# Three rotating 8 MiB buffers, K loaded one pair ahead of V, and the work on head pairs in loops with running address registers

## The chip, the core and the metric

One core of one Trainium2 chip runs the kernel. The metric is the device time of one execution in microseconds. The kernel before takes 654.78 us, the median of six runs (654.01 to 656.37).

## What is computed

A gated mix of two branches for one token x of 512 values: attention over a cache of 32 heads with 16384 keys and values of 128 bf16 numbers each, and a small gated MLP.

```python
g = sigmoid((x * gate_w).sum(-1, keepdims=True))
q = (x @ wq).reshape(B, Sq, H, Dh).transpose(0, 2, 1, 3)      # H = 32, Dh = 128
scores = einsum('bhqd,bhkd->bhqk', q, k_cache) * Dh ** -0.5    # 16384 keys
p = softmax(scores, axis=-1)
o = einsum('bhqk,bhkd->bhqd', p, v_cache)
a = o.transpose(0, 2, 1, 3).reshape(B, Sq, H * Dh) @ wo
z = gelu(x @ w_in); z1 = z[..., :Fh]; z2 = layernorm(z[..., Fh:])
b = (z1 * (w_sp * z2 + b_sp)) @ w_out                          # one token
return g * a + (1 - g) * b
```

The two caches are 128 MiB each, so almost everything that the kernel moves is K and V, and each of their values is used once.

## The kernel before

Heads are taken in 16 pairs. A pair's K fills one buffer of 128 partitions by 64 KiB (8 MiB): head one on partitions 0 to 63, head two on 64 to 127, with 256 keys to a partition. V has the same layout. There are two K buffers (`k_buf`) and one V buffer (`v_buf`); the set-up weights wq and w_in lie in `v_buf`, w_out and a scratch area in `k_buf[1]`, and wo goes into `k_buf[0]` at the end.

For a pair i:

- VectorE multiplies K in place by the query in four chunks of 64 keys (`mult`, L362), each after the load's semaphore (first chunk) and each announced by `mul_s`.
- TensorE sums a chunk's 128 products down to 8 partial sums per key with 16 matmuls against the identity (`scores`, L322 and L74), in one of two PSUM banks. VectorE reduces the 8 to one score (`reduce`, L366).
- ScalarE takes the exponentials of both heads and their sums (`exps`, L378).
- TensorE multiplies the weights into V with 64 matmuls of 8 columns, spread over four column groups of the array (`attend`, L333). ScalarE drains the result to SBUF (L414), and four fp32 matmuls pick the two heads' columns (L339), which ScalarE saves (L416). VectorE inverts the sums (L372).

SyncE's queue issues all large loads in the order K_0, V_0, K_1, V_1, and so on. K_i waits until the scores of pair i-2 are summed (L388), V_i until the V matmuls of pair i-1 are through (L391). The last pair's loads are cut into pieces, K into two and V into three (L398, L402), and after them come five pieces of wo (L421). TensorE's program for two pairs is one loop body with all matmuls written out (L346); VectorE's and ScalarE's programs are written out for all 16 pairs. GpSimd only passes on V's semaphores.

Ahead of the pairs the queries (32 matmuls, L217), the gate, and the MLP branch (16 matmuls L251, a chain of small VectorE steps, 14 matmuls L305) are worked out while the first K loads. After them the outputs are scaled (L424 to L429), turned into columns (L433 to L439, the result is o2), and 64 matmuls of one row by 256 columns multiply by wo (L444) as its pieces land. Two copies and one store end the kernel (L450 to L454).

Of the kernel before, what the change touches and what calls it, by code (L numbers as in the profile page):

```python
# [12 lines left out]
P = 128  # L13
# [17 lines left out]
NG = KP // 4  # L31
ZB = F // 4
K_CUTS = (0, 128, 256)
V_CUTS = (0, 128, 224, 256)
WO_CUTS = (0, 16, 26, 30, 31, 32)
# [3 lines left out]
class Queue:  # L39

    def __init__(self, nc, name):
        self.sem = nc.alloc_semaphore(f"{name}_done")
        self.n = 0
        self.steps = []
# [22 lines left out]
    def issue(self, eng):  # L67
        for step in self.steps:
            step(eng)


def matmul_again(nc, eng, out, lhsT, rhs, **flags):
    with nc.discard():
        ins = eng.matmul(out, lhsT=lhsT, rhs=rhs, **flags).ins  # L74
    return eng.add_instruction(dataclasses.replace(
        ins, name=nc.get_next_instruction_name(), ldweights=False))


def advance(block, engine, n):
    todo = block.instructions  # L80
    loads = [i for i in todo if i.engine == engine and isinstance(i, mybir.InstDMACopy)][:n]
    for load in loads:
        todo.remove(load)
    at = next(j for j, i in enumerate(todo) if i.engine == engine and isinstance(i, mybir.InstDrain))
    todo[at:at] = loads


def gated_mix_kernel(nc, A_x, A_k_cache, A_v_cache, A_wq, A_wo, B_x, B_w_in, B_w_sp, B_b_sp,
# [4 lines left out]
    def ps(name):  # L93
        return nc.alloc_psum_tensor(name, [P, 512], FP32)

    k_buf = [sb(f"k_buf{b}", [P, ROW], BF16) for b in range(2)]
    v_buf = sb("v_buf", [P, ROW], BF16)
    qb = sb("qb", [P, NP * Dh], BF16)
    p_t = sb("p_t", [P, NG * 8], BF16)
    s_sb = [sb(f"s_sb{i}", [P, KP], FP32) for i in range(2)]  # L100
    d_sb = sb("d_sb", [P, 512], FP32)
    x_row = sb("x_row", [1, D], BF16)
# [3 lines left out]
    xgs = sb("xgs", [1, 1], FP32)  # L106
# [19 lines left out]
    L_sb = sb("L_sb", [P, 2], FP32)  # L126
    rl = sb("rl", [P, H], FP32)
    oa = sb("oa", [P, H], FP32)
# [4 lines left out]

    s_ps = [ps(f"s_ps{i}") for i in range(2)]
    d_ps = ps("d_ps")
    o_ps = ps("o_ps")
    l_ps = ps("l_ps")
    a_ps = ps("a_ps")
    m_ps = [ps(f"m_ps{i}") for i in range(2)]
    z_banks = [s_ps[0], s_ps[1], o_ps, l_ps]  # L140

    wq = v_buf[:, 0:DC * HDh]
    w_in = v_buf[:, DC * HDh:DC * (HDh + F)]
    w_out = k_buf[1][:, 0:FhC * D]
    zm = k_buf[1][:, FhC * D:FhC * D + 2 * F].bitcast(FP32)
    wo = k_buf[0]
# [6 lines left out]
    entry = nc.m.functions[0].blocks[0]  # L153
    fin = sem("fin")
    ld_x, ld_g, ld_q, ld_w, ld_u, ld_v, st_out = (
        sem(n) for n in ("ld_x", "ld_g", "ld_q", "ld_w", "ld_u", "ld_v", "st_out"))
    ld_k = [sem(f"ld_k{b}") for b in range(2)]
    ld_kh = [sem(f"ld_kh{b}") for b in range(len(K_CUTS) - 1)]
    ld_vp = [sem(f"ld_vp{b}") for b in range(len(V_CUTS) - 1)]
    ld_o = [sem(f"ld_o{b}") for b in range(len(WO_CUTS) - 1)]  # L160
    mul_s, red_s, sum_s, exp_s, sl_s, pv_s, drn_s, col_s = (
        sem(n) for n in ("mul_s", "red_s", "sum_s", "exp_s", "sl_s", "pv_s", "drn_s", "col_s"))

    pe, dve, act, pool, sp = (Queue(nc, n) for n in ("pe", "dve", "act", "pool", "sp"))
# [5 lines left out]
    for t in [L_sb, p_t]:  # L170
        p_zero = pool.op(lambda e, t=t: e.memset(t[:, :], 0.0), mark=True)
    ones_ok = dve.op(lambda e: e.memset(ones_row[:, :], 1.0), mark=True)
# [18 lines left out]
    for c in range(DC):  # L191
        x_ok = pe.op(lambda e, c=c: e.matmul(
            m_ps[0][:, c * P:(c + 1) * P], lhsT=x_row[0:1, c::DC], rhs=ones_row[0:1, :],
            start=True, stop=True), wait=[(ld_x, 16), ones_ok] if c == 0 else (), mark=True)
    xb_ok = dve.op(lambda e: e.tensor_copy(out=xb[:, :], in_=m_ps[0][:, :]), wait=[x_ok], mark=True)

    for i in range(4):
        dve.chain(lambda e, i=i: e.tensor_copy(
            out=sel[:, i * P:(i + 1) * P].rearrange("h (m i) -> h m i", i=4)[:, :, i],
            in_=ident[0:H, 0:H]), wait=[ident_ok])  # L200
# [6 lines left out]
    xgs_ok = dve.chain(lambda e: e.tensor_reduce(out=xgs[:, :], in_=xg_row[:, :], axis=AX.X,  # L207
                                                 op=ALU.add))

    q_banks = [*z_banks, d_ps, a_ps, m_ps[1], m_ps[0]]  # L210
    q_free = []
    for c in range(DC):
        for n in range(8):
            rhs = wq[:, c * HDh + n * 512:c * HDh + (n + 1) * 512]
            flags = dict(start=(c == 0), stop=(c == DC - 1))
            q_ok = pe.op(lambda e, n=n, c=c, rhs=rhs, flags=flags: (
                e.matmul(q_banks[n][:, :], lhsT=xb[:, c * P:(c + 1) * P], rhs=rhs, **flags)  # L217
                if n == 0 else
                matmul_again(nc, e, q_banks[n][:, :], xb[:, c * P:(c + 1) * P], rhs, **flags)),
                wait=[xb_ok, (ld_q, 16)] if c == 0 and n == 0 else (), mark=(c == DC - 1))  # L220
            if c < DC - 1:
                continue
            for s in range(2):
                rows = slice(64 * s, 64 * s + 64)
                src = q_banks[n][rows, :].rearrange("p (j two d) -> p j two d", two=2,
                                                    d=Dh)[:, :, s, :]
                dst = qb[rows, n * 256:(n + 1) * 256].rearrange("p (j d) -> p j d", d=Dh)
                if n % 2 == 0:
                    ok = dve.op(lambda e, src=src, dst=dst: e.tensor_copy(out=dst, in_=src),  # L229
                                wait=[q_ok] if s == 0 else (), mark=True)  # L230
                else:
                    ok = act.op(lambda e, src=src, dst=dst: e.copy(out=dst, in_=src),
                                wait=[q_ok] if s == 0 else (), mark=True)
            q_free.append(ok)

    pe.op(lambda e: e.matmul(m_ps[1][:, 0:1], lhsT=ones_f[0:1, :], rhs=xgs[:, :], start=True,
                             stop=True), wait=[xgs_ok, q_free[6]], mark=True)
    g_ok = pe.op(lambda e: e.matmul(m_ps[1][:, 1:3], lhsT=ones_row[0:1, :], rhs=wb_row[0:1, :],
                                    start=True, stop=True), wait=[(ld_g, 48)], mark=True)
    act.op(lambda e: e.activation(out=g_sb[:, :], in_=m_ps[1][:, 0:1], func=ACT.Sigmoid),  # L240
           wait=[g_ok], mark=True)
    gm_ok = act.op(lambda e: e.activation(out=gm_sb[:, :], in_=m_ps[1][:, 0:1], func=ACT.Sigmoid,
                                          scale=-1.0), mark=True)
    dve.op(lambda e: e.tensor_copy(out=wbf[:, :], in_=m_ps[1][:, 1:3]), wait=[gm_ok], mark=True)

    for c in range(DC):
        for n in range(4):
            rhs = w_in[:, c * F + n * ZB:c * F + (n + 1) * ZB]
            flags = dict(start=(c == 0), stop=(c == DC - 1))
            z_ok = pe.op(lambda e, n=n, c=c, rhs=rhs, flags=flags: (  # L250
                e.matmul(z_banks[n][:, 0:ZB], lhsT=xb[:, c * P:(c + 1) * P], rhs=rhs, **flags)  # L251
                if n == 0 else
                matmul_again(nc, e, z_banks[n][:, 0:ZB], xb[:, c * P:(c + 1) * P], rhs, **flags)),
                wait=[(ld_w, 16), q_free[2], q_free[3]] if c == 0 and n == 0 else (),
                mark=(c == DC - 1))
            if c == DC - 1:
                m0 = n % 2 * 64
                zb_ok = dve.op(lambda e, n=n, m0=m0: e.tensor_tensor(
                    out=zm[:, n * ZB:(n + 1) * ZB].rearrange("p (m k) -> p m k", k=FhC),
                    in0=z_banks[n][:, 0:ZB].rearrange("p (m k) -> p m k", k=FhC),  # L260
                    in1=ident[:, m0:m0 + 64].unsqueeze(2).broadcast_to([P, 64, FhC]),
                    op=ALU.mult), wait=[z_ok], mark=True)
# [17 lines left out]
    tot_ok = pe.op(lambda e: e.matmul(m_ps[1][:, 0:2], lhsT=ones_f[:, :], rhs=stats[:, :],  # L280
                                      start=True, stop=True), wait=[st_ok, gm_ok], mark=True)
    dve.op(lambda e: e.tensor_scalar(out=mv[:, :], in0=m_ps[1][:, 0:2], scalar1=1.0 / Fh,
# [7 lines left out]
                                          bias=eps_t[:, 0:1], scale=1.0), wait=[var_ok, const_ok],  # L290
                   mark=True)
# [6 lines left out]
                                        op=ALU.mult))  # L298
    u_ok = dve.chain(lambda e: e.tensor_scalar(out=u[:, :], in0=z2n[:, :], scalar1=gm_sb[:, 0:1],
                                               scalar2=0.0, op0=ALU.mult, op1=ALU.add),  # L300
                     wait=[gm_ok])
    d_zero = dve.op(lambda e: e.memset(d_ps[:, :], 0.0), wait=[q_free[4]], mark=True)
    for k in range(FhC):
        for s in range(2):
# [198 lines left out]
```

The softmax here doesn't subtract the row's maximum and nothing guards it: scores larger than these inputs give would overflow.

## Time and profile before

| | before |
|---|---|
| median of six runs | 654.78 us |
| the profiled execution | 654.27 us |
| its span, first to last instruction | 652.5 us |
| mean rate of the transfers over the span | 429 GB/s |
| VectorE multiply L362, 64 times | 282.5 us, 4416 ns each |
| TensorE score matmuls L74 and L322, 1024 times | 275.1 us |
| TensorE V matmuls L333, 1024 times | 68.6 us summed, four at a time |

Busy time is the sum of an engine's instructions. Matmuls that overlap are each counted in full, so a sum on TensorE can be more than the time they took together. The chain of waits follows the work that ended last backwards. SPq and PEq are the sequencers of SyncE and TensorE: they run waits, register operations and branches, and issue the DMAs. "Landing" is the moment at which a DMA's semaphore is complete.

### The profile page before, as it was taken

Reading aid. Unit: us, or ns where it says so; the run is one execution under the profiler, and the core shown is the slowest. Engines: PE = TensorE matmul, PEld = TensorE weight load, DVE = VectorE, ACT = ScalarE, POOL = GpSimd, SP = SyncE. Lnnn points to the kernel's source line nnn. Section 1 sums busy time; section 2 is a strip of 40 time slices with the busy share of each in tenths; the row PEclk is TensorE's granted clock in tenths of the full one; section 3 lists DMA queues with packets and bytes.
Section 4 is the critical chain, followed back from the end, with each engine's and each line's share of the span. In section 5 each row is a group of like instructions: output and inputs, shape, how many; then the busy total and the mean of one; then the engine's idle time right before and its main releaser. Section 6 shows DMA issues by size and latency. Waiting matters only on the chain. (4 is left out here: it accounts for less than half of the span.)

```text
span 652.5 us, 4336 instructions
## 1 busy us (share of the span) xinstructions
PE 374.9 (57%) x2348; PEld 64.5 (10%) x1348; DVE 338.1 (52%) x192; ACT 37.1 (6%) x112; POOL 1.2 (0%) x8
## 2 busy tenths in 40 slices
PE   2646275563837546384563747556484754638766
PEld 0000101011010200102010010101101020010103
DVE  1486290754719166380935629075471915638560
ACT  0210001000010100001010000100001010000100
POOL 0000000000000000000000000000000000000000
PEclk9859788687978959798795978869697895968897
DMA  9999999999999999999999999999999999999997
GB/s 386 478 398 450 443 438 407 442 446 442 406 442 446 430 418 442 446 418 430 442 442 410 438 446 442 410 438 442 446 402 446 442 446 402 442 446 414 426 423 292
DMA packets 6209, 279.64 MB, mean 429 GB/s; under 512 B 696, under 2 KB 956, under 8 KB 1212
## 3 DMA queue, kind: packets, MB, share of 16 engines
q1 hardware_dynamic: 6196, 279.58, 99.3%
q8 instruction: 2, 0.03, 0.0%
q14 instruction: 3, 0.02, 0.0%
q10 hardware_dynamic: 8, 0.00, 0.0%
HBM read 279.58 MB, written 0.00 MB: 429 GB/s over the span
## 5 line engine op out<-in xcount | busy, mean ns | idle before, releaser
L362 DVE TENSOR_TENSOR k_buf<-k_buf,qb 128x8192 bf16<-128x8192 bf16 x64 | 282.5, 4416 | 200.0 <-DMA k_buf<-in_A_k_cache_dram 200.0
L74 PE MATMUL s_ps<-k_buf,ident 128*128 128x512 bf16 x960 | 247.6, 416 | 0.0
L322 PE MATMUL s_ps<-k_buf,ident 128*128 128x512 bf16 x64 | 27.5, 429 | 207.0 <-PEq L315 207.0
L366 DVE TENSOR_REDUCE s_sb<-s_ps 128x64 f32<-128x512 f32 x64 | 44.1, 688 | 74.3 <-PE s_ps L74 74.3
L333 PE MATMUL d_ps<-v_buf,p_t 128*8 128x512 bf16 x1024 | 68.6, 426 | 0.7 <-PEq L330 0.7
L322 PEld LDWEIGHTS s_ps<-k_buf,ident 128*128 128x128 bf16 x64 | 6.3, 98 | 407.2 <-issue 407.2
L378 ACT ACTIVATE p_t<-s_sb 64x256 bf16<-64x256 f32 x32 | 13.3, 414 | 479.7 <-DVE s_sb L366 479.5
L333 PEld LDWEIGHTS d_ps<-v_buf,p_t 128*8 128x8 bf16 x1024 | 30.7, 94 | 30.7 <-issue 13.2
L339 PE MATMUL o_ps<-pick,d_sb 128*128 128x2 f32 x128 | 16.8, 253 | 12.5 <-PEq L337 12.5
L327 PE MATMUL l_ps<-L_sb,ones_f 128*128 128x2 f32 x32 | 5.7, 247 | 30.9 <-PEq L326 30.9
L339 PEld LDWEIGHTS o_ps<-pick,d_sb 128*128 128x128 f32 x128 | 15.9, 195 | 20.1 <-issue 20.1
L327 PEld LDWEIGHTS l_ps<-L_sb,ones_f 128*128 128x128 f32 x32 | 4.8, 188 | 87.2 <-issue 87.2
L414 ACT COPY d_sb<-d_ps 128x512 f32<-128x512 f32 x15 | 8.8, 585 | 71.9 <-PE d_ps L333 71.9
L217 PE MATMUL s_ps<-v_buf,xb 128*128 128x512 bf16 x4 | 2.0, 495 | 9.8 <-DMA v_buf<-in_A_wq_dram 9.8
L444 PE MATMUL a_ps<-k_buf,o 128*1 128x256 bf16 x64 | 5.5, 355 | 0.9 <-DMA k_buf<-in_A_wo_dram 0.9
L378 ACT ACTIVATION_READ_ACCUMULATOR p_t<-s_sb 64x1 f32 x32 | 5.9, 185 | 0.0
L229 DVE CAST qb<-s_ps 64x256 bf16<-64x256 f32 x2 | 0.8, 422 | 7.3 <-PE s_ps L217 7.2
L280 PE MATMUL m_ps<-stats,ones_f 128*128 128x2 f32 x2 | 0.6, 364 | 6.7 <-DVE stats L278 6.7
L205 DVE TENSOR_TENSOR xg_row<-x_row,gw_row 1x512 bf16<-1x512 bf16 x1 | 0.4, 413 | 7.5 <-DMA wb_row<-in_B_b_sp_dram 7.5
L74 PE MATMUL s_ps<-v_buf,xb 128*128 128x512 bf16 (+1 forms) x8 | 3.9, 487 | 0.0
L74 PE MATMUL o_ps<-v_buf,xb 128*128 128x512 bf16 (+1 forms) x8 | 3.9, 487 | 0.0
L444 PEld LDWEIGHTS a_ps<-k_buf,o 128*1 128x1 bf16 x64 | 3.5, 108 | 2.7 <-DMA k_buf<-in_A_wo_dram 1.0
(82 smaller groups left out, 51.6 us busy)
## 6 DMA issues: line engine op xcount, KB each, us to landing
k_buf<-in_A_k_cache_dram SPq DMA_DIRECT2D x2, 4096.0 KB, 39.9
v_buf<-in_A_wq_dram SPq DMA_DIRECT2D x1, 4096.0 KB, 12.2
v_buf<-in_A_v_cache_dram SPq DMA_DIRECT2D x1, 4096.0 KB, 18.5
v_buf<-in_A_v_cache_dram SPq DMA_DIRECT2D x1, 3072.0 KB, 25.4
k_buf<-in_A_wo_dram SPq DMA_DIRECT2D x1, 2048.0 KB, 31.8
v_buf<-in_B_w_in_dram SPq DMA_DIRECT2D x1, 1792.0 KB, 15.4
k_buf<-in_A_wo_dram SPq DMA_DIRECT2D x1, 1280.0 KB, 34.4
v_buf<-in_A_v_cache_dram SPq DMA_DIRECT2D x1, 1024.0 KB, 27.4
```

The lines of the kernel that those rows point to most:

```text
L74: ins = eng.matmul(out, lhsT=lhsT, rhs=rhs, **flags).ins
L217: e.matmul(q_banks[n][:, :], lhsT=xb[:, c * P:(c + 1) * P], rhs=rhs, **flags)
L229: ok = dve.op(lambda e, src=src, dst=dst: e.tensor_copy(out=dst, in_=src), wait=[q_ok] if s == 0 else (), mark=True)
L322: ins = e.matmul(args[0], lhsT=args[1], rhs=args[2], start=True, stop=False)
L327: e.matmul(l_ps[:, 0:2], lhsT=ones_f[:, :], rhs=L_sb[:, :], start=True, stop=True).then_inc(sl_s, 1)
L333: ins = e.matmul(d_ps[32 * g:32 * g + 8, :], lhsT=p_t[:, 8 * t:8 * t + 8], rhs=v_buf[:, t * 512:(t + 1) * 512], start=(t < 4), stop=(t >= ...
L339: ins = e.matmul(o_ps[:, 0:2], lhsT=d_sb[:, r * Dh:(r + 1) * Dh], rhs=pick[:, r * 2:(r + 1) * 2], start=(r == 0), stop=(r == 3))
L362: dve.op(lambda e: e.tensor_tensor(out=k3, in0=k3, in1=q3, op=ALU.mult), wait=wait, inc=(mul_s, 1))
L366: dve.op(lambda e: e.tensor_reduce(out=s_sb[i % 2][:, c * QK:(c + 1) * QK], in_=s_ps[c % 2][:, :].rearrange("p (j w) -> p j w", w=W), axis ...
L378: act.op(lambda e, s=s, rows=rows: e.activation(out=p_t[rows, :].rearrange("p (t c) -> p t c", c=8)[:, :, 4 * s:4 * s + 4], in_=s_sb[i % 2 ...
L414: act.op(lambda e: e.copy(out=d_sb[:, :], in_=d_ps[:, :]), wait=[(pv_s, i + 1), d_zero], inc=(drn_s, 1))
L444: y_ok = pe.op(lambda e, k=k, s=s: e.matmul(a_ps[32 * s:32 * s + 1, 0:256], lhsT=o2[:, k:k + 1], rhs=wo[:, k * D + s * 256:k * D + (s + 1) ...
```

## The change

K and V share three buffers in rotation. The loads run K_0, K_1, V_0, K_2, V_1, and so on to K_15, V_14, V_15, wo; load n goes into buffer n mod 3 and waits until the user of load n-3 is done. The set-up weights all lie in the third buffer. GpSimd waits for every load and hands it on through two counting semaphores, `k_s` and `v_s`.

TensorE's order becomes scores(0), scores(1), values(0), scores(2), values(1), and so on, in blocks that branch to each other. Scores run in loops of four chunks by five groups of three matmuls, values in a loop of 16 groups of four. Buffer addresses are kept in registers (`kw`, `va`, `pa`) that are advanced in the loop, with one register operation ahead of each matmul. VectorE's and ScalarE's programs for pairs are loops as well. The V matmuls now add onto a bank that is zero at the start of a pair: ScalarE drains it and then copies zeros into it (`renew`). The outputs of all pairs gather in one PSUM bank, and the softmax sums are summed over the partitions once, at the end. Before the pairs, the query and MLP matmuls are loops that add onto banks cleared by VectorE. The first 28 of wo's 32 slices are multiplied as rows of 512 columns in four column groups, then copied to SBUF and summed by two fp32 matmuls; wo comes in seven pieces.

```diff
-    k_buf = [sb(f"k_buf{b}", [P, ROW], BF16) for b in range(2)]
-    v_buf = sb("v_buf", [P, ROW], BF16)
+    bufs = sb("bufs", [P, 3 * ROW], BF16)
+    buf = [bufs[:, b * ROW:(b + 1) * ROW] for b in range(3)]
...
+    k_at = [max(2 * i - 1, 0) for i in range(NP)]
+    v_at = [min(2 * i + 2, 2 * NP - 1) for i in range(NP)]
+    setup = buf[v_at[0] % 3]
...
+    dve.op(lambda e: e.memset(ps_all[:, 0:7 * 512], 0.0), mark=True)
...
+    z_zero = dve.op(lambda e: e.memset(ps_all[:, 0:4 * 512], 0.0), wait=[q_free[3]], mark=True)
...
+    u_ok = dve.op(lambda e: e.memset(ps_all[:, 4 * 512:6 * 512], 0.0), wait=[q_free[5]], mark=True)
...
+    def scores(e, i, ka, kw):
+        take(e, exp_s)
...
+        with e.Fori(0, NQ) as c:
+            e.reg_mov(kw, ka)
+            take(e, mul_s)
...
+            with e.Fori(0, 5) as v:
+                kv = k3[:, :, bass.ds(v * (3 * W) + W, 3 * W)]
+                for w in range(3):
+                    ins = matmul_on(nc, e, lambda: matmul_again(
+                        nc, e, s3, ident[:, :], kv[:, :, w * W:(w + 1) * W], start=False, **flags),
+                        [(kw, 2 * W * (w + 1))])
+                e.reg_alu(kw, kw, 6 * W, ALU.add)
+                ins.then_inc(sum_s, 1)
...
+    def values(e, p, pa, va):
...
+        with e.Fori(0, NT) as t:
+            take(e, v_s)
+            p8 = p_t[:, bass.ds(t * (TG * 8), TG * 8)]
+            v8 = bufs[:, bass.ds(t * (TG * 512), TG * 512)]
+            for j in range(TG):
+                ins = matmul_on(nc, e, lambda: matmul_at(
+                    nc, e, d_ps, 32 * (j % 4), (8, 512), p8[:, 8 * j:8 * j + 8],
+                    v8[:, j * 512:(j + 1) * 512], (p_t[:, 0:8], bufs[:, 0:512])),
+                    [(va, 1024 * j), (pa, 16 * j)])
+            ins.then_inc(pv_s, 1)
+            e.reg_alu(va, va, 2 * TG * 512, ALU.add)
+            e.reg_alu(pa, pa, 2 * TG * 8, ALU.add)
+        take(e, drn_s)
...
+    def renew(e):
+        drain(e).then_inc(zer_s, 1)
+        take(e, zer_s)
+        e.copy(out=d_ps, in_=zero[:, :]).then_inc(drn_s, 1)
...
+    for n, kind, i in loads:
+        wait = [user[n - 3]] if n >= 3 else [w_free] if buf[n % 3] is setup else []
...
+    def hand(e, loaded, to, n):
+        take(e, loaded, 16)
+        e.nop().then_inc(to, n)
...
-WO_CUTS = (0, 16, 26, 30, 31, 32)
+WO_CUTS = (0, 8, 16, 24, 28, 30, 31, 32)
+WIDE = 28
...
+            if k < WIDE:
+                wide_ok = pe.op(lambda e, k=k: e.matmul(
+                    s_ps[0][32 * (k % 4):32 * (k % 4) + 1, :], lhsT=o2[:, k:k + 1],
+                    rhs=wo[:, k * D:(k + 1) * D], start=(k < 4), stop=(k >= WIDE - 4)), wait=wait,
+                    mark=(k == WIDE - 1))
+                continue
...
+        if b == H - 2:
+            w_ok = act.op(lambda e: e.copy(out=d_sb[:, :], in_=s_ps[0]), wait=[wide_ok], mark=True)
```

`matmul_on` emits a matmul and replaces its address arithmetic by one addition to the running register; neighbouring register operations (two additions here, one for each operand) are fused into one instruction by the compiler. `matmul_at` places a matmul on a given column group.

## The prediction

> **What bounds the kernel now.** I read the page's busy shares and queues first, then SyncE's waits, then the chain of waits, then the last 50 us in the timeline and by line.
>
> ```profile
> span 652.5 us, 4336 instructions
> PE 374.9 (57%) x2348; PEld 64.5 (10%) x1348; DVE 338.1 (52%) x192; ACT 37.1 (6%) x112; POOL 1.2 (0%) x8
> ...
> q1 hardware_dynamic: 6196, 279.58, 99.3%
> q8 instruction: 2, 0.03, 0.0%
> q14 instruction: 3, 0.02, 0.0%
> ```
>
> No engine is above 57%, while SyncE's queue keeps the 16 DMA engines at work for 99.3% of the span. The kernel is a stream of 279.58 MB. Two thin rows below it are instruction fetches, five packets in the span.
>
> ```profile
> SPq L391 <- PE d_ps L333: 522.4, 14, 40.7
> ```
>
> SyncE waits nearly always for V's buffer (the end of L333). That wait costs no transfer: the first K half of the last pair is used at 610.68 and the next V is issued at 611.63, when the second half of that K is still in flight (a K takes 47.2 us from issue to landing; pairs follow at 155.54 - 116.84 = 38.7 us in the timeline, so one K or V is 19.35). So the queue never runs dry, and a third buffer has no bubble to fill.
>
> ```profile
> 612.47 0.43 SPq L402
> 612.90 0.04 issue
> 612.95 31.82 DMA k_buf<-in_A_wo_dram
> 644.77 0.04 issue
> 644.81 5.55 PE a_ps L444 x64
> 650.36 0.02 issue
> 650.39 0.41 DVE res L450
> ```
>
> The end: wo's first piece lands at 644.77, the 64 matmuls of L444 run up to 650.36. By L421's landing times (35 us after issues up to 614.85) the last piece lands at about 649.8, so TensorE ends only 0.6 us after the stream.[...]
>
> ```profile
> 639.98 0.14 PEld L333 LDWEIGHTS d_ps<-v_buf,p_t 128*8 128x8 bf16 x8 [1.13 <-issue]
> 640.01 0.61 PE L333 MATMUL d_ps<-v_buf,p_t 128*8 128x512 bf16 x8 [0.66 <-PEq L330]
> 640.66 0.58 ACT L428 COPY d_sb<-d_ps 128x512 f32<-128x512 f32 x1 [4.93 <-PE d_ps L333]
> ...
> 644.00 0.19 DVE L439 CAST o<-m_ps 128x32 bf16<-128x32 f32 x1 [0.40 <-PE m_ps L436]
> ```
>
> V's last piece lands at 639.9 and is used within 0.7 us. From the drain to o2 is 644.2 - 640.65 = 3.6 us. One pair's 64 V matmuls take 3.63 us in the timeline (the row at 607.96): 57 ns each, since four share the array.
>
> ```profile
> L346 PEldq ALU_OP  x8: 36/36/39, 108.0 to 641.4; - x8
> L346 PEldq COMPARE_BRANCH  x8: 76/208/214, 108.1 to 641.5; - x8
> ```
>
> These rows (the line of the old loop) hold the prices of the new loops: a register operation runs 36 ns, a taken branch 208 ns. In the trace the branch starts 97 ns after the register operation before it started, so one register operation occupies the sequencer for 97 ns. A semaphore wait there (L315, L326) runs 51 ns and the next instruction starts 75 ns after it.
>
> [...]
>
> **The change, part by part.**
>
> 1. Load order and buffers. K one pair ahead; load n waits for load n-3's user. In steady state V_i needs K_i's exponentials, about 25 us after K_i landed (116.84 to 142 in the timeline), and has two loads, 38.7 us. K_i needs V_(i-3) used, also with 38.7 us. Cost 0. The narrow place is V_1, which waits for the second exponentials. DVE's set-up gains memsets: at L302's 485 ns per 512 columns, 2048 columns are 1.9 us and 1024 are 1.0, both on the chain; all four z products now wait for the last matmul, about +1. DVE starts K_0 at about 43.3 instead of 39.23. Two pairs follow at 24.7 (39.23 to 63.92) and 23.2 us (no half-clock first chunk): exponentials at 92, V_1 needed when K_2 ends at about 96 (18.7 us of set-up loads and four loads of 19.4). Margin 3 us, cost 0; the bound is a bubble of up to 3 us.
>
> 2. Scores in loops. Per three matmuls (3 x 214 = 642 ns at full clock) the sequencer has 3 ALU, 1 fused register instruction, 1 branch: 4 x 97 + 208 = 596 ns plus pushes. Level with the array; with the outer loop about 4.3 us a chunk, under VectorE's 4.93 us a chunk (592.63 to 597.56). Cost 0, hidden by VectorE.
>
> 3. Values in loops. Per four matmuls (213 ns of array): 1 wait 75, 4 fused register instructions and 1 for the running addresses at 97 each = 485, branch 208 = 768 ns, plus 64 before the branch (as from 36 to 97 in that row): 832 ns. The fused form and matmuls with register addresses are not in the trace.[...] I take t = 0.83 us; 16 iterations are 13.3 us against 3.63.
>  In mid-stream TensorE's pair is then 4 chunks from its own start (about 18 us, VectorE having two products ready) + 13.3 + 2.7 for drain, zero copy and L459 = 34 us < 38.7. Hidden by the stream.
>
> 4. The tail. The last loads are V_14, V_15, wo. V_15 lands at 639.9 and V_14 19.4 us earlier, 620.5. Values(14) runs 620.5 to 633.8; hand-over 2.7 (drain 0.58, the new copy of zeros about 0.5, L459's matmuls 1.0, semaphores and branches); values(15) 636.5 to 649.8, where before the last V matmul ended at 640.6. Then 0.3 for the last matmuls, 3.6 to o2: 653.7. Then 28 wide matmuls at 57 ns and latency 1.8, ACT's copy 0.6 and semaphores, two fp32 sums (not in the trace; 0.3 to 1.0, I take 0.6): +3.2, y at 656.9 against 650.35. In short y = 630.3 + 32 t. The wide matmuls win nothing back: 64 at 54 ns are 3.5, the new chain is 3.2. TensorE may start values(14) 0.4 late behind scores(15). Sum 656.9 - 650.35 + 0.4 = +6.9.
>
> 5. Instruction fetch. The code shrinks[...]. In the trace's landing marks of wo's last piece 12 engines are done by 648.1 and four trail up to 649.8; the trailing began after fetches at 44.6, 71.0, 107.6. Fewer fetches give back 0 to 1.6 us; I take -0.6.
>
> 6. Small. One branch per engine before its first DMA, +0.1. POOL now hands on every landing (in order, one instruction of about 0.05 and propagation): 0.15 us on each, on the path only for V_15; anything queued behind a POOL wait lands later anyway. ACT's exps(i) queues behind the drain of pair i-2, which ends before scores(i) starts. SyncE's loads queue behind each other's waits in landing order. Reciprocals (16 x 0.17), oa copies (15 x 0.16) and 30 sum matmuls go, all under the stream: 0.
>
> Sum: +6.9 - 0.6 + 0.1 = +6.4 on the profiled execution's 654.27 (span 652.5 and 1.8 around it): 660.7. The median of six runs is 654.78, 0.5 above, so 661.2.
>
> **Rivals.**
> (a) Not slower: the sequencer hides its work. Below t = 0.63 values(15) ends by 643.5, o2 is ready before wo's last pieces, and the tail is the stream's again. Then part 5 decides: with one or no fetch left, -1.4, giving 653; with the fetches still there and the fp32 sums late, 654.5. For it: the old loop's ALU_OP ran under queued matmuls. Against: 7 control instructions for 213 ns of array leave nothing queued to hide under.
> (b) TensorE becomes the bound in every pair. From t = 1.1 (18 + 16 t + 2.7 > 38.7) each further 0.1 us costs 1.6 us per pair, 15 pairs: t = 1.2 gives about +24 and a tail of +17, near 690 to 700. For it: unpriced register addresses, and the score loop already level with the array. Against: 97 ns is measured.
> (c) The start starves: exponentials of pair 1 late by more than 3 us; a bubble of 1 to 5 us, 655 to 660 alone. Small.
>
> **Numbers.** About 0.2% (1.3 us) is what a measurement tells from no change. Forecast 0.54 (c included), (b) 0.18, (a) faster 0.18, (a) unchanged 0.10. So faster 0.18, same 0.10, slower 0.72. The forecast's own range is 656 (t = 0.67) to 671 (t = 1.05). The range for 8 in 10 takes in (a) faster down to 652.5 and half of (b), up to 685.
>
> **What would show it.** Right: in the timeline a pair's 64 V matmuls (ps_all<-bufs,p_t) take 12 to 15 us; DMA share stays near 99% to about 640 and the chain of waits ends in these matmuls, ACT's drain and L606 instead of the wo transfer; o2 is cast after 650. Wrong: if 64 V matmuls take under 10 us and the chain still ends in wo's DMA. If DMA's GB/s dips once a pair, (b); if it dips only near 95 us, (c).

## The result, and the profile after

The changed kernel takes 696.57 us (median of ten runs, 695.14 to 697.71), the kernel before 654.32 in the same comparison (twenty runs). The ratio is 1.0643, with a 95% interval of 1.0634 to 1.0652: slower by 42 us where 7 had been predicted. One execution of the run setup_written_out below, 712.84 us at a granted clock of 0.873, fell in a slower state of the chip and is left out of its ratio; the other three took 687.53 to 692.61 at 0.910 to 0.919.

The page of the changed kernel, with the rows that answer to those shown of before:

```profile
span 695.7 us, 8611 instructions
...
PE 506.2 (73%) x2293; PEld 113.5 (16%) x1293; DVE 344.2 (49%) x181; ACT 44.2 (6%) x113; POOL 2.1 (0%) x9
...
GB/s 388 437 471 426 422 305 422 422 396 441 369 422 414 430 433 411 433 430 441 433 426 414 433 426 418 422 426 448 418 445 407 441 433 418 413 428 422 406 84 0
...
q1 hardware_dynamic: 6484, 279.58, 94.2%
q14 instruction: 1, 0.01, 0.0%
```

The same bytes move, but the stream fills 94.2% of the span where it filled 99.3%. TensorE is the engine that grew (375 to 506 us), and the program executes twice as many instructions (8611, before 4336). The row of rates shows the two main places of the loss: one dip near 96 us (305), and two almost empty slices at the end (84 and 0). One instruction fetch is left of five.

The busy times count a stretch in which several matmuls overlap only once, unlike what the text under the table of before says: the 1024 V matmuls have a mean of 381 ns each, 390 us in all, and are listed with 188.2 us busy, where the page of before lists 68.6.

Windows of the span give those places in numbers (the window and its length; PE, PEld, DVE, ACT, POOL busy; granted clock, DMA share, GB/s by the start of each packet):

```profile
80.00:100.00 20.00, 16.67 (x66) 0.82 (x10) 13.75 (x8) 1.01 (x4) 0.00 (x0) 0.86 0.74 318
94.00:96.00 2.00, 2.00 (x11) 0.10 (x1) 0.69 (x1) 0.00 (x0) 0.00 (x0) 1.00 0.18 66
96.00:98.00 2.00, 1.92 (x9) 0.00 (x0) 0.00 (x0) 0.00 (x0) 0.00 (x0) 1.00 0.00 0
98.00:100.00 2.00, 1.00 (x7) 0.53 (x7) 1.69 (x2) 1.01 (x4) 0.00 (x0) 1.00 0.00 0
640.00:660.00 20.00, 15.38 (x68) 3.15 (x38) 7.27 (x5) 1.01 (x4) 0.00 (x0) 0.91 0.99 412
660.00:680.00 20.00, 15.20 (x79) 7.09 (x79) 1.09 (x3) 1.18 (x2) 0.00 (x0) 0.83 0.23 92
680.00:695.00 15.00, 10.07 (x77) 4.49 (x77) 1.01 (x4) 1.54 (x3) 0.00 (x0) 0.89 0.00 0
```

In the transfer records the last packet of wo ends at 665.9 us, before at 649.3. So of the 43.3 us by which the span grew, 16.6 are a stream that ends later, and 26.7 are work behind it (29.8 us against 3.1). Of the 16.6, the dip is about 5.5 (from 88 to 104 us a mean of 284 GB/s, with each packet spread over its duration, where 434 flow otherwise): no packet starts from 96 to 100 us. The rest, some 11, is spread thinly over the later pairs.

The chain of waits no longer ends in a transfer (start, duration, work):

```profile
686.69 1.06 PE ps_all L459 x8
...
689.19 2.75 PE ps_all L606 x28
691.93 0.02 issue
691.96 0.59 ACT d_sb L618
692.55 0.04 issue
692.60 0.82 PE ps_all L620 x4
693.42 0.24 PE ps_all L612 x4
693.65 0.02 issue
693.68 0.41 DVE res L624
```

TensorE works through V_15 and wo long after both have landed. In mid-stream one pair looks like this in the timeline (16 rows of V matmuls, of which three are shown):

```profile
336.36 0.69 DVE L491 TENSOR_REDUCE s_sb<-ps_all 128x64 f32<-128x512 f32 x1 [2.78 <-DVEq L81]
...
337.02 0.72 PE L98 MATMUL ps_all<-bufs,p_t 128*8 x4 [0.81 <-PEq L81]
...
338.01 0.74 PE L98 MATMUL ps_all<-bufs,p_t 128*8 x4 [0.27 <-PEq L81]
...
352.00 0.72 PE L98 MATMUL ps_all<-bufs,p_t 128*8 x4 [0.28 <-PEq L81]
352.85 0.59 ACT L527 COPY d_sb<-ps_all 128x512 f32<-128x512 f32 x1 [14.46 <-ACTq L81]
353.55 0.59 ACT L532 CAST ps_all<-zero 128x512 f32<-128x512 bf16 x1
...
355.83 0.61 PE L427 MATMUL ps_all<-bufs,ident 128*128 x1
356.23 4.56 PE L85 MATMUL ps_all<-bufs,ident 128*128 x15
...
360.95 0.69 DVE L491 TENSOR_REDUCE s_sb<-ps_all 128x64 f32<-128x512 f32 x1 [10.60 <-DVEq L81]
361.56 4.42 DVE L506 TENSOR_TENSOR bufs<-bufs,qb  x1
...
371.39 0.39 PE L427 MATMUL ps_all<-bufs,ident 128*128 x1 [1.08 <-PEq L81]
371.62 3.63 PE L85 MATMUL ps_all<-bufs,ident 128*128 x15
...
376.06 0.76 PE L98 MATMUL ps_all<-bufs,p_t 128*8 x4 [0.81 <-PEq L81]
```

From V loop to V loop are 39.0 us (337.02 to 376.06): 15.8 for the 64 V matmuls, a new group of four every 1.00 us; 3.0 for the hand-over (drain, copy of zeros, four small products); 20.2 for the scores. None of these overlaps another, and the stream brings a pair in 38.7. The scores are not TensorE's alone: VectorE stands 10.6 us in front of its reduce of chunk 0 (360.95), and the last two products of K come behind that reduce.

The next pair takes 39.5 us, and the two lengths alternate from the third pair on; the first two take 40.6 and 40.7. The mean from V loop 0 (98.74) to V loop 14 (651.08) is 39.5. Windows on the scores of the pair shown (chunks 0 and 1) and of the next (chunks 0 and 2) show where they differ, in the granted clock:

```profile
356.00:360.60 4.60, 4.60 (x16) 0.10 (x1) 0.00 (x0) 0.00 (x0) 0.00 (x0) 0.72 1.05 442
361.00:365.50 4.50, 3.25 (x16) 0.00 (x0) 4.50 (x2) 0.00 (x0) 0.00 (x0) 1.00 1.04 451
395.00:399.60 4.60, 4.60 (x14) 0.01 (x1) 0.00 (x0) 0.00 (x0) 0.00 (x0) 0.63 1.02 442
406.20:411.00 4.80, 4.80 (x16) 0.10 (x1) 4.15 (x1) 0.00 (x0) 0.00 (x0) 0.64 1.01 437
```

At a clock of 1.00 a chunk takes TensorE 3.45 us (16 matmuls, one every 0.216 in chunk 1). Chunk 0 takes 4.80 in the pair shown and 5.16 in the next. An estimate from these: with chunk 0 at 1.00 both pairs would take 37.7 to 37.8 us and lie under the stream's 38.7. No run holds the clock, so this is not shown.

### The profile page after: what moved, and what is told of

Same layout as the page of the kernel before. It is cut to its first block, busy times and chain, and to the rows that moved or that the text cites. A ratio compares the mean times of both kernels' runs of the same rounds, so it can differ in the third digit from the quotient of the medians.

```text
span 695.7 us, 8611 instructions
## 1 busy us (share of the span) xinstructions
PE 506.2 (73%) x2293; PEld 113.5 (16%) x1293; DVE 344.2 (49%) x181; ACT 44.2 (6%) x113; POOL 2.1 (0%) x9
## 3 DMA queue, kind: packets, MB, share of 16 engines
q1 hardware_dynamic: 6484, 279.58, 94.2%
## 5 line engine op out<-in xcount | busy, mean ns | idle before, releaser
L506 DVE TENSOR_TENSOR bufs<-bufs,qb x64 | 281.5, 4419 | 53.9 <-DVEq L81 53.9
L85 PE MATMUL ps_all<-bufs,ident 128*128 x960 | 261.4, 429 | 0.0
L98 PE MATMUL ps_all<-bufs,p_t 128*8 x1024 | 188.2, 381 | 75.4 <-PEq L81 75.0
L491 DVE TENSOR_REDUCE s_sb<-ps_all 128x64 f32<-128x512 f32 x64 | 44.1, 689 | 230.6 <-DVEq L81 230.6
L98 PEld LDWEIGHTS ps_all<-bufs,p_t 128*8 x1024 | 83.9, 82 | 231.3 <-issue 203.5
L427 PE MATMUL ps_all<-bufs,ident 128*128 x64 | 27.0, 422 | 53.4 <-PEq L81 50.5
L459 PE MATMUL ps_all<-pick,d_sb 128*128 128x2 f32 x128 | 19.4, 273 | 26.9 <-PEq L81 26.9
L518 ACT ACTIVATE p_t<-s_sb 64x256 f32 (+1 forms) x32 | 13.3, 414 | 341.3 <-ACTq L81 340.9
L527 ACT COPY d_sb<-ps_all 128x512 f32<-128x512 f32 x16 | 9.4, 586 | 235.1 <-ACTq L81 235.1
L459 PEld LDWEIGHTS ps_all<-pick,d_sb 128*128 128x128 f32 x128 | 18.1, 217 | 31.6 <-issue 31.6
L85 PE MATMUL ps_all<-bufs,xb 128*128 x40 | 13.8, 491 | 0.0
L289 PE MATMUL ps_all<-bufs,xb 128*128 x4 | 2.0, 500 | 7.8 <-DVE xgw L274 7.8
L329 PE MATMUL ps_all<-bufs,xb 128*128 x4 | 2.3, 574 | 3.6 <-DVE ps_all L317 3.6
## 6 DMA issues: line engine op xcount, KB each, us to landing
bufs<-in_B_w_in_dram SPq DMA_DIRECT2D x1, 1792.0 KB, 15.7
```

Of the source, the lines that this page charges most:

```text
L98: ins = eng.matmul(bank[0:m, 0:n], lhsT=lhsT, rhs=rhs, **flags).ins
L329: e.matmul(args[0], lhsT=args[1], rhs=args[2], **flags))
L427: matmul_on(nc, e, lambda: e.matmul(s3, lhsT=ident[:, :], rhs=k3[:, :, 0:W], start=True, **flags), [(kw, 0)])
L459: ins = e.matmul(o2, lhsT=d_sb[:, r * Dh:(r + 1) * Dh], rhs=pick[:, r * 2:(r + 1) * 2], start=False, stop=False, skip_group_check=True)
L491: return e.tensor_reduce(out=s_sb[:, c * QK:(c + 1) * QK], in_=s_ps[c % 2].rearrange("p (j w) -> p j w", w=W), axis=AX.X, op=ALU.add)
L506: e.tensor_tensor(out=k3, in0=k3, in1=qi, op=ALU.mult).then_inc(mul_s, 1)
```

## The experiments

All change the changed kernel, but for one that changes the kernel before. Times are medians, ratios against the kernel before in the same comparison.

| run | us | ratio (95%) |
|---|---|---|
| v_pass_of_8 | 666.28 | 1.0181 (1.0164 to 1.0198) |
| v_pass_of_2 | 831.78, one run | |
| scores_written_out | 675.69 | 1.0339 (1.0321 to 1.0356) |
| pairs_written_out | 658.05 | 1.0056 (1.0040 to 1.0073) |
| before_with_v_loop | 698.38 | 1.0664 (1.0635 to 1.0693) |
| v_16_scores_written_out | 659.97 | 1.0094 (1.0077 to 1.0111) |
| v_16_scores_setup_written_out | 655.05 | 1.0014 (1.0007 to 1.0022) |
| pairs_and_setup_written_out | 656.58 | 1.0032 (1.0020 to 1.0044) |
| setup_written_out | 692.49 | 1.0542 (1.0510 to 1.0575) |
| v_16_setup_short_tail | 655.90 | 1.0018 (1.0007 to 1.0030) |
| v_16_setup_short_tail_score_loop | 655.54 | 1.0013 (1.0003 to 1.0023) |
| v_16_setup_end_written_out | 655.61 | 1.0024 (1.0017 to 1.0030) |

**The size of a V pass.** Two runs change only how many V matmuls stand in one pass of the loop.

```diff
-TG = 4
+TG = 8    # v_pass_of_8
+TG = 2    # v_pass_of_2
```

> The V loop takes 8 passes of 8 matmuls instead of 16 of 4; every value and the order of loads stay. In the trace of the changed kernel a pass of 4 lasts 1.00 us: 0.15 from the semaphore wait to the first register instruction, 3 x 0.115, 0.135, 0.11, and 0.26 from the branch to the next wait. Theory A (TensorE's serial sum of scores, V loop and hand-over is the bound): a pass of 8 lasts 1.46, a pair's V work 11.7 instead of 16, TensorE's pair 34.9 instead of 39.05, below the stream's 38.7. Then the stream sets the middle again and only the late start (about 5 us) and the tail are left: 659 to 666 us. Theory B (the order of loads in three buffers leaves the transfers waiting): nothing in it changes, 690 to 697. Theory C (the score loop's overhead is what fills TensorE): it still takes its 20.2 us, but with 4.3 us less per pair behind it also C gives a gain; C differs in the run with the score loop written out.

> The V loop takes 32 passes of 2 matmuls. Theory A: a pass lasts 0.15 + 0.115 + 0.135 + 0.11 + 0.26 = 0.77 us, 32 are 24.6 against 16, so each of 16 pairs is 8.6 us longer and nothing hides it: 696.6 + 138 = 835 us (825 to 845). Theory B: the transfers wait for other things, 697 to 720.

The timeline of v_pass_of_8 has a pass of eight every 1.46 us:

```profile
631.48 1.20 PE L98 MATMUL ps_all<-bufs,p_t 128*8 x8 [0.27 <-PEq L81]
...
632.94 1.20 PE L98 MATMUL ps_all<-bufs,p_t 128*8 x8 [0.26 <-PEq L81]
```

A pass of two takes 0.76 us. A pair's V loop is then 8 x 1.46 = 11.7 or 32 x 0.76 = 24.3 us against 16.0. The small pass costs 8.3 us more in each of 16 pairs, 133 us; 135 were measured. The large one brings the pair under the stream's 38.7 us (4.3 us less in each), and 30 of the 42 us are gone, just short of what was expected. What is left is a stop of the stream from 96.5 to 101.4 us and 10.8 us of work behind the last packet of wo. In mid-stream TensorE's serial work, with VectorE's products in its chain, sets the time of the changed kernel.

**Writing out.** First the inner score loop alone, then all of TensorE's pair work (no registers, no branches; the three buffers, the order of loads and the other engines' loops stay).

```diff
-            with e.Fori(0, 5) as v:
...
+            for w in range(1, NS):      # scores_written_out
+                ins = matmul_on(nc, e, lambda: matmul_again(nc, e, s3, ident[:, :],
+                    k3[:, :, w * W:(w + 1) * W], start=False, **flags), [(kw, 2 * W * w)])
+            ins.then_inc(sum_s, 1)
...
-        with e.Fori(0, NT) as t:
+        for t in range(NT):             # pairs_written_out, scores likewise
```

> The inner loop of the scores (5 passes of 3 matmuls) is written out as 15 matmuls, each still with its register operation; the V loop stays. Theory A: the score matmuls are paced by the array (chunk 0 at half clock, 4.9 us) and by VectorE (4.93 us a chunk); only the last chunk's 3.63 us shrinks to 3.4 and the way out of the loops by up to 0.3: 0.3 to 0.6 us per pair, 687 to 692 us. Theory C (the score loop's sequencer work fills TensorE): 4 chunks lose about 1 us each, 4 us per pair: below 670 us.

> TensorE's work on pairs is written out for all 16 pairs with fixed addresses: no register operation and no branch in it. The three buffers, the order of loads, scores one pair ahead of V, VectorE's, ScalarE's and GpSimd's loops, and the set-up loops stay. Theory A: V work takes 3.6 us again, TensorE's pair about 26; the stream is the bound, what stays is the late second exponentials (bubble of 4 to 5 us near 95 us) and a level tail: 655 to 661 us, with some of it instruction fetches for about 200 KB of code. Theory B: the order of loads costs as before, over 685 us.

scores_written_out gained 21 us, between the two expectations. Its timeline shows where: the V loop now begins 3.55 us after the start of the last chunk, where it was 4.67 (371.39 to 376.06), and its first two passes take 1.37 us together (321.68 to 323.05), where they took 1.99.

```profile
318.13 0.39 PE L427 MATMUL ps_all<-bufs,ident 128*128 x1 [1.26 <-PEq L81]
318.35 3.40 PE L85 MATMUL ps_all<-bufs,ident 128*128 x15
...
321.68 1.10 PE L98 MATMUL ps_all<-bufs,p_t 128*8 x8
...
323.05 0.72 PE L98 MATMUL ps_all<-bufs,p_t 128*8 x4 [0.26 <-PEq L81]
```

The pair falls from 39.0 to 37.5 us (one V issue to the next, 323.42 to 360.96). It stays there for eight pairs, until TensorE has caught up with the stream, which then sets the pace again. From V loop 0 to V loop 14 are 531.6 us, where they were 552.3: this is the gain of 21. I had thought the score loop free. pairs_written_out takes the 64 V matmuls back to 3.63 us, fetches 0.26 MB of instructions in 16 packets (15 of 0.25 MB on q8, one of 0.01 on q14), and loses 0.56% against the kernel before, so the order of loads, the third buffer and the other engines' loops cost little; its chain of waits ends in the wo transfer again (622.78, 29.51 us).

**The loops without the buffers.** The kernel before, with its V matmuls in a loop:

```diff
-            for t in range(a // 4, b // 4):
...
+            with e.Fori(max(a // 16, 1), b // 16) as t:    # 4 per pass, running va and pa
```

> The kernel before with its two K buffers, one V buffer and load order, in which only the 64 V matmuls of a pair are put in a loop of 4 per pass with running address registers (no semaphore per pass). Theory A (TensorE's serial register work is the cost): a pass is the 1.00 us of the changed kernel less its semaphore wait, about 0.83 us, so the V matmuls take about 13 us where they took 3.6, 9.5 us more; from the trace of before about 8 us of that fit between V's freeing and the end of the load ahead of it, so the stream stalls 1 to 3 us in each of some 14 pairs: 668 to 700 us. Theory B (the loss needs the changed load order or the third buffer): within 3 us of before.

698.38 us: the V loop alone makes the kernel before as slow as the whole change makes it. A pass without the semaphore takes 0.89 us. The timeline shows what the old buffers do with it:

```profile
361.85 0.33 SPq L450 DMA_DIRECT2D v_buf<-in_A_v_cache_dram  x1
361.86 0.59 ACT L473 COPY d_sb<-d_ps 128x512 f32<-128x512 f32 x1 [13.89 <-PE d_ps L86]
362.22 0.43 SPq L447 DMA_DIRECT2D k_buf<-in_A_k_cache_dram  x1
...
364.08 4.42 DVE L421 TENSOR_TENSOR k_buf<-k_buf,qb 128x8192 bf16<-128x8192 bf16 x1 [17.16 <-DMA k_buf<-in_A_k_cache_dram]
```

The one V buffer comes free only at 361.85, K waits in SyncE's queue behind it, and VectorE stands 17 us for K (15 to 18 in the pairs of mid-stream, where the kernel before has 13 to 15). Six V issues from 241.1 to 445.8 are 40.9 us apart, so the stream loses 2.2 us in each pair. In this state the changed buffers and load order together are worth something: a mean of 39.5 against 40.9, although the pass with the semaphore is the longer one.

**The remainder: the set-up.** With V passes of 16 and the score matmuls written out, the set-up's loops and clears are left. (All runs with passes of 16 also move one cut of the last V load, from 224 to 192 keys, as a pass then covers 64.)

```diff
-        with e.Fori(0, DC) as c:         # queries, gMLP; mixer likewise
+        for c in range(DC):              # with start=(c == 0): no clears ahead of them
...
-    dve.op(lambda e: e.memset(ps_all[:, 0:7 * 512], 0.0), mark=True)
-    z_zero = dve.op(lambda e: e.memset(ps_all[:, 0:4 * 512], 0.0), wait=[q_free[3]], mark=True)
-    u_ok = dve.op(lambda e: e.memset(ps_all[:, 4 * 512:6 * 512], 0.0), wait=[q_free[5]], mark=True)
+    b_zero = dve.op(lambda e: e.memset(ps_all[:, 2 * 512:6 * 512], 0.0), wait=[q_free[5]], mark=True)
```

> The changed kernel with V passes of 16 matmuls (about 2.38 us each, 9.5 us a pair) and the inner score loop written out. Theory A: a pair takes 18.7 + 9.5 + 2.9 = 31 us on TensorE, under the stream's 38.7, so what is left over before is the late V_1 of the start and two V phases of the tail that are 6 us longer each than written out ones: about 658.5 us (655 to 662). Theory D (something else of the change holds the stream as well): over 664.

> As v_16_scores_written_out, with the query, gMLP and mixer matmuls written out too and with four banks cleared once, beside the tail of the mixer's input, instead of eight at three places. If the set-up loops and clears are what delays V_1 (99 us in the changed kernel, about 92 needed): K_0's first product near 40 us instead of 45.5, V_1 issued near 93, no dip of the stream between 80 and 100 us, and 2 to 4 us less than v_16_scores_written_out, about 655 (653 to 658). If V_1 is late for another reason: within 1 us of v_16_scores_written_out.

> As pairs_written_out (658.05 us), with the set-up matmuls written out as well. The stream then dips nowhere: 1.2 us of bubble less and up to 1 us of earlier start: 656.5 (654.5 to 658). Under 654 only if the changed load order itself is worth something against the kernel before.

> The changed kernel with its pair loops as they are, and only the set-up matmuls written out with the clears joined into one. K_0's first product moves from 45.5 to about 40 us and the dip of the stream between 80 and 100 us goes. As TensorE is the bound from there on, everything behind moves by as much: 4 to 6 us off 696.6, 691.5 (690 to 693). If the pairs' lateness swallows the start (the pairs wait for something else than their own turn on TensorE): within 1 us of 696.6.

All four came as their first theory said: 659.97, 655.05, 656.58, 692.49. In setup_written_out VectorE starts K_0 at 39.33 (45.53 in the changed kernel), V_1 is issued at 92.01 (99.42), and the window of the dip is full:

```profile
80.00:100.00 20.00, 15.27 (x68) 3.16 (x38) 10.31 (x6) 1.01 (x4) 0.00 (x0) 0.91 0.98 423
```

That is worth 4.1 us by the medians with the pairs' loops in place, 4.9 us with the large passes. v_16_scores_setup_written_out keeps three buffers and loops and is 0.14% behind the kernel before.

**Is the score loop dear in itself?** The two short-tail runs differ in that loop alone; both take the set-up above, passes of 16 and a smaller wide part of the last product.

```diff
-WIDE = 28
+WIDE = 16
...
-        if b == H - 2:
+        if b == 24:
```

> As v_16_scores_setup_written_out (655.05 us), with the wide part of the last product cut from 28 to 16 heads and its copy and two sums placed ahead of the last four pieces of wo. In the profile of that run the last pieces land at 649.6 and TensorE, ScalarE, TensorE then need 2.77 us one after the other (0.62, 0.59, 1.02, 0.44 and the gaps); 16 narrow matmuls behind the landing need about 1.15 us by the pace of the kernel before (two in 0.109 us, 0.27 for the last): 1.6 us less, 653.4 (652.5 to 654.4), under the 654.2 of the kernel before. If the end is set by another thing than this chain: 655 as before.

> As v_16_setup_short_tail, but with the inner score loop of the changed kernel put back (its 5 passes of 3). Between after and scores_written_out this loop was worth 21 us. Theory A (TensorE's serial time counts only where it is above the stream's period): a pair is 20.2 + 9.5 + 2.9 = 32.6 us, still 6 us under 38.7, so the loop now costs nothing: within 1 us of v_16_setup_short_tail. Theory E (the score loop costs its 1.5 us in each pair whatever else holds): 17 to 23 us more.

With and without the loop: 655.54 and 655.90. The loop that was worth 21 us is worth nothing here. By the terms above a pair takes 20.2 + 9.5 + 3.0 = 32.7 us (9.5 from 319.71 to the drain at 329.23); its first two V loops, for which TensorE does not wait for the stream, start 31.7 us apart. The timeline of the run with the loop shows the V passes of 16, 2.42 us apart:

```profile
322.12 2.16 PE L98 MATMUL ps_all<-bufs,p_t 128*8 x16 [0.30 <-PEq L81]
...
324.54 2.16 PE L98 MATMUL ps_all<-bufs,p_t 128*8 x16 [0.26 <-PEq L81]
```

The shorter tail itself brought nothing (655.05 without it), where 1.6 us had been expected. A last attempt also wrote out the V matmuls of the last two pairs:

```diff
+        with nc.body("pe_last", valid_engines=kind):
+            values_once(e, NP - 2)
...
+            values_once(e, NP - 1)
```

> As v_16_setup_short_tail, with the V matmuls of the last two pairs written out. In the profile of v_16_setup_short_tail (655.9 us, single runs 653.6 to 657.4) the last V matmul is issued at 642 and the wo product begins at 645.9, so 3 us of matmuls still lie behind the landing of wo near 649. Written out the two V phases are 12 us shorter: the wo product keeps up with its landings and only the last pieces lie behind them: 653.3 (652.5 to 654.3), at or just under the kernel before. If the landing of wo alone sets the end: 655 to 656.

655.61: a miss. Its chain of waits still ends in TensorE (the wo product begins at 645.95 and runs to 651.27, before 644.81 to 650.36). Single runs of the short-tail versions lie between 653.6 and 657.4, those of before in the same comparison between 653.8 and 656.8; what decides within that spread was not found. No version beat the kernel before.

## Why the prediction was wrong

The direction was right, the size was not. What came is rival (b), "TensorE becomes the bound in every pair", given 0.18; rival (c), the bubble at the start, came with it. That (b)'s 690 to 700 us hold the result is in part luck: they were worked out for t = 1.2, as 24 us in the pairs and 17 in the tail. A pass took 1.00 us, for which (b)'s own sum finds no loss in the pairs; the measured parts are 16.6 (5.5 of them the bubble) and 26.7.

- **The step that failed is part 3**, the sum "4 chunks from its own start (about 18 us, VectorE having two products ready) + 13.3 + 2.7 [...] = 34 us < 38.7. Hidden by the stream." Measured: 20.2 + 15.8 + 3.0 = 39.0, and 39.5 in every second pair. Two terms are mis-sized.
  - The V loop was t = 0.83 and is 1.00 us. In the sequencer's records of the changed kernel's trace, as means of 240 passes, the next instruction starts 151 ns after the start of the wait (75 assumed), the four fused operations with their two pushes take 122, 118, 115 and 119 to the start of the next (97), the one for the running addresses 115 to the branch (97), the branch 260 to the next wait (208, and 64 that were put ahead of it): 151 + 474 + 115 + 260 = 1000 ns (979 to 1025 in single passes).
  - The scores were 18 and are 20.2. Chunk 0 runs at a granted clock of 0.72, in the next pair at 0.63, and VectorE's third product is queued behind the reduce of chunk 0. The kernel before shows the slow first chunk too (15 matmuls in 5.44 us at 586.55, granted clock 0.62 from 586.2 to 592.0).
- **The cliff of rival (b) was set at t = 1.1** by the same 18. With the measured terms it is at (38.7 - 20.2 - 3.0) / 16 = 0.97. The prediction's own range (to t = 1.05) thus lay on both sides of the edge while it was priced as one slope. The terms of 18 and 2.7 had no bounds; t alone had a range, an estimate of the author's.
- **Being a little slower than the stream was enough to lose 26.7 us at the end.** V loop 0 starts at 98.7 and V loop 14 at 651.1: 39.5 us a pair, 0.8 above the stream's 38.7, 11 us in 14 pairs, which is the thin loss of the stream. TensorE never catches up the lateness that it starts with. Part 4 let V_14's landing start the tail, at 620.5; it was the end of the scores of K_15, at 651.1. From there the formula is right: t = 1.00 gives 36.4 + 32 x 0.17 = 41.8 us to y, measured 42.6 (651.1 to 693.7). v_pass_of_8, with t = 0.73, gives 33.2 and measures 33.9 (630.0 to 663.9).
- **Part 2, "Cost 0, hidden by VectorE", was wrong by 1.5 us a pair.** VectorE hides three chunks (TensorE waits 2.21 and 1.08 us for the products of chunks 2 and 3 in the pair shown); getting out of the loops behind the last one is on the path (4.67 us from the start of the last chunk to the V loop, 3.55 with the inner loop written out). It is free only where the pair has slack, which the two short-tail runs show (655.54 us with the loop, 655.90 without). The 214 ns of a score matmul and the 213 of four V matmuls are 216 in the trace of before.
- **Part 1's margin of 3 us was wrong, its bound of "a bubble of up to 3 us" too.** V_1 was issued at 99.42, not 92, and 5.5 us of the stream went. Of the 7.4 us, 2.2 are the start: the first K_0 product begins at 45.53 where 43.3 was estimated. Most of the rest is in the two pairs, which take 53.4 us up to the second exponentials (45.53 to 98.88) where 24.7 + 23.2 = 47.9 were counted. The mixer's looped matmuls hold TensorE from 46.0 to 51.0, so the first scores begin at 52.04. And the second pair has a slow first chunk after all (15 matmuls in 5.43 us at 78.01, granted clock 0.62 from 78.0 to 83.4), which "no half-clock first chunk" had ruled out, and a slow third one (4.79 at 89.53, clock 0.68 from 89.5 to 94.0). Written out, the set-up lets K_0 start at 39.33 and V_1 at 92.01, in time, although the two pairs still take 52.1.
- With the load order, the buffers and the loops of the other engines alone, 0.32% are lost (pairs_and_setup_written_out, 2.4 us): "Cost 0" was near, and where that rest lies was not traced.
- **Parts 5 and 6** do not show in the time: nothing in the end of the changed kernel waits for a transfer. One fetch is left (at 61.7), but the landing marks of wo's last piece still lie 1.88 us apart (664.40 to 666.29), before 2.14 (647.63 to 649.77): that fewer fetches give the trailing back was not shown.

The price of a branch held: the V and score loops of the changed kernel's trace have 201 to 209 ns taken and 69 to 76 at the exit, before 208 and 76. Rival (a) had for it that the old loop's ALU_OP "ran under queued matmuls". In the trace of before it starts at 107.956 and the branch at 108.056, while five of the eight matmuls ahead of them start from 108.239 on. In the V pass at 339.92 of the changed kernel each fused operation but the first starts 29 ns behind the weight load ahead of it, and each starts 86 ns before its own (340.036 after 340.007, before 340.122). The prediction's own test, dips of the rate once a pair for (b), hardly shows in 40 slices; the share of 94.2% and the empty end do.

## What to carry to other kernels

Where two paces are close, price every term of the pair's chain with bounds, not only the one that changes, and ask on which side of the equality each end lies. Under it the score loop cost nothing; over it, by 0.8 us a pair, the start's lateness was kept, grew, and was paid at the end. The V loop with running addresses cost a fixed 0.53 us for each pass, so the size of a pass was the first thing to set (16 matmuls a pass, 9.5 us a pair, not 4 with 16.0). Code ahead of a stream's first dependent load counts even when the rest is slower: here K_0's products began 6.2 us earlier and the kernel gained about 4. And a TensorE term needs its granted clock, read from the trace for the stretch that it stands for (a chunk of scores took 3.45 us at 1.00, and 4.80 and 5.16 as chunk 0).

## What was not expected of the hardware

- The time of a V pass is a straight line in its matmuls: 0.76, 1.00, 1.46, 2.42 us for 2, 4, 8, 16, about 0.53 us + 0.12 us each. Written out, in the kernel before, they take 57 ns each: four start within 10 ns, and the next four 216 ns after them. So even without the fixed part a matmul with two running addresses goes at half the pace: in the sequencer's records of the changed kernel 115 ns (the median) pass from one fused register operation, over the pushes of a weight load and a matmul, to the next.
- A take of a semaphore in the changed kernel's V loop runs 51 ns, but the next register operation starts 151 ns after its start (in before, 76 ns to the next weight load); in before_with_v_loop, without a take, the pass is 0.89 instead of 1.00 us.
- The same score loop was worth 21 us in one setting (696.57 and 675.69) and nothing in another (655.54 with it, 655.90 without).
- The granted clock is low again in chunk 0 of every pair (0.72 and 0.63 in the windows above; in the first of them 0.50 from 355.2 to 358.5 and 1.00 from 358.7 on), right behind a V loop that ran at 1.00 with TensorE busy in 11.7 of 15.7 us (window 337.0 to 352.7). What brings it down was not tested.
